# Local and pooled attention with a gated feed-forward on one core: the last product in float16, its scale from a per-batch bound, tails of two batches together, the pooled attention on quadrants of TensorE

## The chip, the cores and the metric

One core of a Trainium2 chip runs the program. The metric is the device time in microseconds (us), the median of several runs. A profile of one execution shows every instruction of its engines: TensorE (PE, with its weight loads PEld), VectorE (DVE), ScalarE (ACT), GpSimd (POOL) and SyncE (SP), which starts the transfers.

## What is computed

Batch B = 8, heads H = 8, sequence S = 576, head dimension D = 64. The attention's output is the input of a gated feed-forward; the outputs of the two attentions are added first.

```python
q_d, k_d, v_d = (mean over 4 neighbouring positions of q, k, v)      # 144 positions
out_up = repeat(softmax(scale * q_d @ k_d.T) @ v_d, 4)               # pooled attention
scores = where(abs(pos[:, None] - pos[None, :]) < 4, scale * q @ k.T, -1e9)
x = out_up + softmax(scores) @ v                                     # local attention
h = maximum(x @ w_in, 0)                                             # 512 -> 1024
u, v = h[..., :512], h[..., 512:]
v_n = (v - mean(v)) / sqrt(var(v) + 1e-6)
v_s = einsum('ts,bsd->btd', w_spatial, v_n) + b_spatial[None, :, None]
out = (u * v_s) @ w_out
```

The weights w_in and w_out come as 64-bit floats and are taken apart as integers on the chip.

## The kernel before

**Two kinds of work.** `attention(n)` handles unit n, a pair of heads of one batch (32 units, four to a batch). `gated(b)` handles the feed-forward of batch b. Neither runs as written: each piece is handed to a planner (`Plan`) as an operation with an engine, an assumed duration, its buffers and a rank. The planner then writes out one fixed order for each engine, and every engine works through its own list in that order. So a changed duration, rank or buffer count moves instructions everywhere. Tables of numbers (`RANK`, `MRANK`, `WRANK`) hold the ranks; `ON` says for each unit which engine does a piece that several can do.

**A unit.** S: the local scores, ten windows of 64 by 64 for each of the two heads, as 20 float32 products that each use one quadrant (64 rows by 64 columns) of TensorE's array (L663). Then mask, maximum, subtraction, exponential, sum and division on VectorE, ScalarE or GpSimd. T turns the probabilities (L716), AV multiplies by v, again 20 products on quadrants (L796). The pooled half: two additions make the sums of four (L631, L634); Sd, the pooled scores, is three float32 products that use the whole array, with the two heads laid out in a matrix padded with zeros (qd, L638, L728); Td turns the probabilities (L764); AVd is four products that use one half of the array's columns each (L782). L806 adds the two attentions into xf, and x is xf split into two float16 parts, high and low (L814, L816).

**A batch's feed-forward.** V (L844, the last 64 rows L849), U (L899) and SP, the spatial product (L917 to L920), are float16 products of 12 to 14 matmuls; each sums high times high, high times low and low times high. g = u * v_s is split into two float32r parts (L930, L924), and O, the last product (L947), is 12 matmuls of 512 columns in float32r for every 128 rows of the output. The last 64 rows of each batch make a product of 8 matmuls of their own (L952): high and low rows stand under each other and two further instructions add them (L959, L960).

**Start.** The weights are decoded by six operations for each of 12 pieces (L453 to L478), their size is bounded (L401 to L415), and they are split (L426, L429). x needs the scale of its batch, which needs all of v of the batch. TensorE has no weights for V until then. Where the planner expects a gap on TensorE in the first 110 us, it fills it with matmuls whose result nobody reads (L985).

Of the kernel before, what the change touches and what calls it, by code (L numbers as in the profile page):

```python
# [23 lines left out]
NW = len(WS)  # L24
# [29 lines left out]
class Op:  # L54
    __slots__ = ("eng", "ns", "fn", "rank", "lag", "port", "kb", "mode", "succ", "wait", "ready", "bufs", "name", "way")
# [14 lines left out]
TURN = {"FQ": 93.0, "FH": 93.0, "QF": 120.0, "QH": 100.0, "HF": 200.0, "HQ": 200.0, "FF": 0.0, "QQ": 20.0, "HH": 0.0}  # L70
# [6 lines left out]
class Plan:  # L77
# [18 lines left out]

    def op(self, eng, ns, fn, r=(), w=(), hold=(), after=(), rank=0.0, lag=None, port=False, kb=0, mode="",
           name=""):
# [8 lines left out]
        o.mode = mode  # L107
# [24 lines left out]
    def run(self, near=150.0, stay=0.0, dma=(1500.0, 4.2, 500.0), emit=True):  # L132
# [4 lines left out]
        moved = 0.0  # L137
        next_of = {t: 0 for t in self.places}
# [10 lines left out]
        while left:  # L149
            best = None  # L150
            for eng, ops in todo.items():
                t0 = free[eng]
                first, found = None, []
                for o in ops:
# [14 lines left out]
                    if ok:  # L169

                        ask = t
# [42 lines left out]
            if o.kb:  # L214
                moved = max(moved, t + dma[0]) + o.kb * dma[1]

                stop = t + dma[0] + 2 * o.kb * dma[1] + 2 * dma[2] if o.eng == "POOL" else moved + dma[2]
# [22 lines left out]
RANK = {"load": [-2.065, -19.673, -22.423],  # L240
        "vload": [14.683, -10.412, -19.503],
        "vabs": [1.439, 2.3, -51.738],
        "tv": [-29.16, -7.708, 15.837],
        "sum": [-11.259, -21.094, 21.557],
        "S": [-37.552, -7.505, 7.145],
        "E": [-6.056, 0.92, -0.304],
        "N": [-1.928, 0.973, 7.716],
        "T": [-13.789, 4.31, -7.205],
        "Sd": [-6.836, 6.538, 1.368],
        "Nd": [-13.355, -14.998, -2.48],  # L250
        "Td": [-12.97, -17.495, 0.215],
        "AVd": [-13.065, -3.029, 0.094],
        "AV": [9.436, 0.605, -3.631],
        "X": [-0.741, 3.256, -1.768]}
# [12 lines left out]
NEAR = 109.698
STAY = 7.379
# [15 lines left out]
def tile_kernel(ctx, tc, qk, vw, v4, w_in, wT, bsp, w_out, out, emit=True):  # L284
# [34 lines left out]
    for par in range(2):  # L319
# [7 lines left out]
    rebias = const.tile([P, 1], F32, name="rebias")  # L327
    nc.gpsimd.memset(rebias, -7.0 * 2.0**30)
# [5 lines left out]


# [7 lines left out]
    plan.tag("g", [const.tile([P, NF, 2 * HN], F32R, name="ga"),  # L343
                   lambda: const.tile([P, NF, 2 * HN], F32R, tag="gb", name="gb")])
# [17 lines left out]
    places("ed", 2, [96, 3, G], F32)
    places("mxd", 2, [P, 3], F32)
    places("smd", 2, [P, 3], F32)
    places("pdT", 1, [72, 2, 3, 96], F32)
# [13 lines left out]
    sw = const.tile([P, 3, 16], F32, name="sw")  # L379
    places("mb", 5, [P, FF], F32)  # L380
    places("wst", NT + 1, [P, S], F32)
    places("bias", 1, [P, S], F32)
    places("row", 5, [P, FF], F32, fifo=False)
    places("u", 5, [P, HN], F32)
# [3 lines left out]
    PEL = 260  # L388

# [4 lines left out]
    def bound(t, k, toks, tok, rank, up, fac, low):  # L394

# [4 lines left out]
        def turn_b():  # L400
            nc.tensor.transpose(pb.ap[:k, :P], t()[:, :k], ident)  # L401

        def greatest():
            nc.vector.tensor_reduce(t()[:k, 10:11], pb.ap[:k, :P], axis=AX.X, op=ALU.max)

        def spread():
            nc.tensor.matmul(pb.ap[:, P:P + 1], ones[:k], t()[:k, 10:11], start=True, stop=True)

        def scales():
            e, sc, iv = (t().bitcast(I32)[:, i:i + 1] for i in (7, 8, 9))  # L410
            nc.vector.tensor_copy(t()[:, 7:8], pb.ap[:, P:P + 1])
# [619 lines left out]
```

## Time and profile before

| | |
|---|---|
| median of 3 runs | 594.53 us (593.16 to 594.92) |
| profiled execution, from the first to the last instruction | 593.0 us |
| TensorE busy | 571.2 us, 96% |
| VectorE / ScalarE / GpSimd busy | 440.1 / 351.3 / 88.1 us |
| TensorE's granted clock, mean | 0.996 of full speed |
| moved by DMA | 56.95 MB |

The profile gives no time for its own execution beside the span; the span is 1.5 us under the median of the runs. Busy time counts overlapping matmuls' durations only once, and a matmul's shown duration is longer than the distance to the next one, because they are pipelined. So what a product costs TensorE is read here from start to start.

### The profile page before, as it was taken

The numbers are of one execution on the slowest core, as the hardware profiler recorded it, in microseconds if no ns is written. First come the engines' busy times: TensorE is split into PE (matmuls) and PEld (weight loads), VectorE is DVE, ScalarE is ACT, GpSimd is POOL, SyncE is SP. The second block draws the span as 40 slices with busy tenths as digits, with TensorE's granted clock in tenths as the row PEclk, the third lists the DMA queues.
The fourth block names the chain that finished last, engine by engine and source line by source line (L and its number), as shares of the span: only waits on it lengthen the run. The fifth ranks groups of instructions, "written<-read, shape, count | busy, mean of one in ns | idle before, by whom it ended". The sixth has DMA issues, their size and how long they took to land.

```text
span 593.0 us, 14813 instructions
## 1 busy us (share of the span) xinstructions
PE 571.2 (96%) x6062; PEld 420.0 (71%) x6062; DVE 440.1 (74%) x1077; ACT 351.3 (59%) x886; POOL 88.1 (15%) x109
## 2 busy tenths in 40 slices
PE   7777899999999999999999999999999999999997
PEld 3444558786788668776888678776787678766775
DVE  5889999987885968796687947797687957554340
ACT  3798998666656465665656555665656445533421
POOL 3212464002200040003100210003100110001100
PEclk9999999999999999999999999999999999999999
DMA  8999714215341623144140442144130110001002
GB/s 271 230 309 238 200 27 99 77 34 155 60 151 38 166 57 122 33 145 102 40 126 34 133 103 98 48 146 88 55 125 10 74 49 34 2 19 45 19 1 80
DMA packets 37383, 56.95 MB, mean 96 GB/s; under 512 B 3650, under 2 KB 24130, under 8 KB 37316
## 3 DMA queue, kind: packets, MB, share of 16 engines
q1 hardware_dynamic: 35012, 48.94, 26.2%
q0 software_dynamic: 2304, 7.08, 7.4%
q8 instruction: 47, 0.77, 0.5%
q14 instruction: 20, 0.16, 0.1%
HBM read 46.57 MB, written 9.44 MB: 94 GB/s over the span
## 4 chain that ended last, share of the span: by engine, by line
PE 84%; DVE 5%; ACT 4%; DMA 3%; issue 2%; POOL 0%; ACTq 0%; DVEq 0%; POOLq 0%
PE pmc L917 4%; PE pmc L844 4%; PE pmd L899 4%; PE pmb L947 4%; PE pmb L917 4%; PE pma L899 4%; PE pmb L844 4%; PE pmd L917 4%; PE pmd L947 4%; PE pmc L947 4%; PE pma L917 4%; PE pmc L899 3%; PE pma L947 3%; PE pmb L899 3%; PE pab L796 2%; PE pma L844 2%
## 5 line engine op out<-in xcount | busy, mean ns | idle before, releaser
L899 PEld LDWEIGHTS <-win 128*128 128x128 f16 x768 | 74.4, 98 | 19.5 <-issue 1.5
L917 PEld LDWEIGHTS <-vha 128*128 128x128 f16 x768 | 73.8, 98 | 19.4 <-issue 1.7
L581 POOL DMA_DIRECT2D tvb<-v_dram x12 | 10.3, 857 | 126.2 <-DMA tvb<-v_dram 102.9
L917 PE MATMUL pmc<-wsp,vha 128*128 128x320 f16 (+1 forms) x204 | 28.6, 290 | 0.0
L985 PE MATMUL pma<-mask_b,mask_a 128*128 128x512 bf16 x91 | 24.7, 417 | 3.2 <-DVE sw L506 3.2
L917 PE MATMUL pmb<-wsp,vha 128*128 128x320 f16 (+1 forms) x192 | 27.1, 291 | 0.0
L581 POOL DMA_DIRECT2D tva<-v_dram x12 | 10.8, 902 | 101.3 <-DMA tva<-v_dram 56.8
L917 PE MATMUL pmd<-wsp,vha 128*128 128x256 f16 (+1 forms) x192 | 24.9, 279 | 0.0
L917 PE MATMUL pma<-wsp,vha 128*128 128x256 f16 (+1 forms) x180 | 24.0, 283 | 0.0
L872 POOL TENSOR_TENSOR sta<-sta,mhalf 128x1 f32<-128x1 f32 (+1 forms) x14 | 11.2, 803 | 78.9 <-DVE sta L856 72.3
L872 POOL TENSOR_TENSOR stc<-stc,mhalf 128x1 f32<-128x1 f32 (+1 forms) x13 | 11.0, 845 | 67.7 <-DVE stc L856 67.5
L676 DVE TENSOR_TENSOR sa<-pab,mask 128x384 f32<-128x384 f32 (+1 forms) x24 | 10.5, 480 | 11.9 <-PE pab L663 11.8
L985 PEld LDWEIGHTS <-mask_a 128*128 128x128 bf16 x97 | 9.4, 104 | 13.8 <-issue 3.6
L704 ACT ACTIVATE sa<-sa 128x640 f32<-128x640 f32 x16 | 11.8, 735 | 11.8 <-DVE sa L682 11.8
L947 PE MATMUL pmd<-wo,ga 128*128 128x512 f32 x72 | 18.1, 399 | 0.0
L947 PE MATMUL pma<-wo,gb 128*128 128x512 f32 x72 | 18.0, 399 | 0.0
L844 PEld LDWEIGHTS <-xa 128*128 128x128 f16 x96 | 9.3, 98 | 11.8 <-issue 1.1
L947 PEld LDWEIGHTS pmd<-wo,ga 128*128 128x128 f32 x72 | 13.3, 188 | 3.0
L947 PEld LDWEIGHTS pma<-wo,gb 128*128 128x128 f32 x72 | 13.3, 188 | 3.0
L947 PE MATMUL pmb<-wo,ga 128*128 128x512 f32 x60 | 15.1, 401 | 0.0
L872 POOL TENSOR_TENSOR stb<-stb,mhalf 128x1 f32<-128x1 f32 (+1 forms) x13 | 10.7, 826 | 23.4 <-DVE stb L856 23.1
L806 DVE TENSOR_TENSOR xfa<-pab,dna 128x232 f32<-128x232 f32 x32 | 11.2, 391 | 2.8 <-ACT win L426 1.7
(730 smaller groups left out, 1653.2 us busy)
## 6 DMA issues: line engine op xcount, KB each, us to landing
qka<-qk_dram SPq DMA_DIRECT2D x16, 576.0 KB, 3.8
qkb<-qk_dram SPq DMA_DIRECT2D x16, 576.0 KB, 6.2
tva<-v_dram POOLq DMA_DIRECT2D x12, 288.0 KB, 4.4
tvb<-v_dram POOLq DMA_DIRECT2D x12, 288.0 KB, 4.4
out_dram<-rowb SPq DMA_DIRECT2D x9, 256.0 KB, 2.0
stg<-w_in_dram SPq DMA_DIRECT2D x4, 512.0 KB, 4.8
more<-w_in_dram SPq DMA_DIRECT2D x4, 512.0 KB, 9.8
out_dram<-rowa SPq DMA_DIRECT2D x7, 256.0 KB, 2.0
```

What stands on the lines that cost most here:

```text
L581: plan.op("POOL", 850, lambda r=r: nc.gpsimd.dma_start(t.ap, v4[b, r], accum_op=ALU.add), w=[t], rank=rank + 2.0 + 0.3 * r, kb=288, name="tv")
L676: nc.vector.tensor_tensor(sv, pv, mask[:, None, None, :].broadcast_to(list(pv.shape)), op=ALU.add)
L704: exp_of.append(plan.op("ACT", 643, lambda: nc.scalar.activation(s.ap, s.ap, AF.Exp, scale=1.0 / 8.0), w=[s], rank=R["E"], name="exp"))
L796: nc.tensor.matmul(pv.ap[h * 64:h * 64 + 64, c:c + QB[w + 1] - QB[w]], vb.ap[k, w], pT.ap[k, blk, q0:q0 + QB[w + 1] - QB[w]], start=True, ...
L806: nc.vector.tensor_tensor(xo[:, :, o], pj[:, o, :m].rearrange("p (j g r) -> p j g r", j=2, r=4), do[:, :, o, :, None].broadcast_to([P, 2, ...
L844: nc.tensor.matmul(ps.ap, xs[c].ap[:, i, t * P:(t + 1) * P], win[:, c, j, FF:], start=(c == 0 and (i, j) == (0, 0)), stop=(c == NC - 1 and ...
L872: plan.op("POOL", 530, lambda: nc.gpsimd.tensor_tensor(st.ap[:r, 8:9], st.ap[:r, 8:9], mhalf[:r], op=ALU.pow), w=[st], rank=rank - EVICT, ...
L899: nc.tensor.matmul(ps.ap[:, :n], win[:, c, i, ft * P:(ft + 1) * P], xs[c].ap[:, j, HA[h]:HA[h + 1]], start=(c == 0 and (i, j) == (0, 0)), ...
L917: nc.tensor.matmul(ps.ap[:, :n], vh.ap[:, c, i, fs], wsp[:, c, j, hs], start=(c == 0 and (i, j) == (0, 0)), stop=False)
L947: nc.tensor.matmul(ps.ap, g.ap[:, c, o1:o1 + P], wo[:, c, j, :], start=(c == 0 and (i, j) == (0, 0)), stop=(c == NF - 1 and i == 1))
L985: nc.tensor.matmul(ap.rearrange("p (j k) -> p j k", k=64), mask_a, mask_b[:, None, :].broadcast_to([P, 8, 64]), start=True, stop=True)
```

## The change

**Last product.** w_out is kept as two float16 parts instead of float32r, and so is g. float16 needs g in a bounded range. A new bound per batch does this: the ReLU that makes u also sums its rows (`accum_out`, L1105), VectorE takes the largest of the eight sums, TensorE turns that column, VectorE takes its maximum, TensorE spreads it over the partitions with a product with ones, and three small VectorE operations make two scales. The gate (L1155) multiplies by one, and the copy of the output (L1174) by the other.

**Tails.** The last 64 rows of g of two batches go into one buffer `gt`, and after every second batch `o_tails` multiplies both by w_out in 12 matmuls.

**Pooled attention.** Sd becomes six products on quadrants, without the padded qd and without its two scaling copies. AVd becomes eight products on quadrants with an addition of the two halves. Td turns 112 instead of 96 columns. From unit 8 on S and Sd are one piece of the plan, and AVd and AV are one.

**Others.** The decoding takes four operations instead of six. For 18 of 32 units the subtraction of the maximum moves into ten exponentials of 64 columns each. More work goes to GpSimd. The sizes of w_spatial's columns are summed by ten matmuls (L642). The first four qk tiles have buffers of their own. All ranks and assumed durations are new, with one rank per batch and, for the first two batches, per unit.

```diff
-    wo = const.tile([P, NF, 2, E], F32R, name="wo")
+    wo = const.tile([P, NF, 2, E], F16, name="wo")
...
-        plan.op("PE", 720, scores_d, r=[kb, qb.sub(0), qb.sub(1)], w=[pd], hold=[ed], rank=R["Sd"], lag=PEL, mode="F", name="Sd")
...
+            q = kb.ap.rearrange("p x g -> p (x g)")
+            for h, a, i, e in ((0, 0, 0, 0), (0, 1, 1, 0), (1, 1, 0, 2), (1, 2, 1, 2), (0, 2, 0, 1), (1, 0, 1, 1)):
+                r, o = slice(h * 64, h * 64 + 64), slice(i * 64, i * 64 + 64)
+                nc.tensor.matmul(third(e)[o], q[r, a * 48:a * 48 + 64], kb.ap[r, 1], start=True, stop=True)
...
+        merge = n >= MERGE
...
+            second = plan.op(Way("mask", n, T=("PE", 1710, False), D=("PE", 1242, False)), 0, lambda: (scores(), scores_d()), r=[qkb, kb], w=[pst, pdt, pe],
+                             hold=[s, ed], rank=R["S"], lag=PEL, mode="Q", name="S")
...
-                    nc.tensor.matmul(pw.ap[h * 64:h * 64 + 64, :G], vd[:, kc * 2 + h, :], t[:, kc, :, h, :],
+            for kc in range(2):
+                for c, h in ((0, 0), (1, 1), (0, 1), (1, 0)):
+                    k = slice(c * 64, KEYS if c else 64)
+                    nc.tensor.matmul(bank(two_w, c ^ h)[h * 64:h * 64 + 64, base[c ^ h]:base[c ^ h] + G], vd[k, kc * 2 + h, :], t[k, kc, h * G:h * G + G],
                                      start=(kc == 0), stop=(kc == 1))
...
+            plan.op("ACT", 480 if h == 0 else 535, lambda: nc.scalar.activation(u.ap[:, :n], ps.ap[:, :n], AF.Relu, scale=iv.ap[:, 1:2], accum_out=au.ap[:, h * NF + ft:h * NF + ft + 1]),
...
+                turned.append(bound(lambda: au.ap, 1, [au.sub(8), ("sw", 2), ("sw", 3)], au.sub(9), rank, scales, 480))
...
-            plan.op("DVE", 341 if h == 0 else 407, lambda: nc.vector.scalar_tensor_tensor(u.ap[:, :n], ps.ap[:, :n], sw[:, 2, 9:10], u.ap[:, :n], op0=ALU.mult, op1=ALU.mult),
-                    r=[ps], w=[u], rank=rank - EVICT, name="gate")
+            plan.op("DVE", 395 if h == 0 else 460, lambda: nc.vector.scalar_tensor_tensor(u.ap[:, :n], ps.ap[:, :n], au.ap[:, 9:10], u.ap[:, :n], op0=ALU.mult, op1=ALU.mult),
+                    r=[ps, au.sub(9)], w=[u], rank=rank - EVICT, name="gate")
...
+        def o_tails():
...
+                for c in range(NF):
+                    for i, j in PAIRS:
+                        nc.tensor.matmul(ps.ap, gt.ap[:, c, i].rearrange("p s t -> p (s t)"), wo[:, c, j, :],
+                                         start=(c == 0 and (i, j) == (0, 0)), stop=(c == NF - 1 and i == 1))
...
-        for ft in range(NF):
-            s_piece(0, ft)
-            u_piece(1, ft)
+        for h in range(2):
+            for ft in range(NF):
+                u_piece(h, ft)
```

TensorE's list, in the middle of a batch before: Td, S of two units, AVd, then SP (pa and pm are accumulators, qk the loaded heads, pdT the turned pooled probabilities, tv the pooled v).

```order
L764 MATMUL pmb<-ident,eda 72x96 x3
L764 MATMUL pma<-ident,eda 72x96 x3
L663 MATMUL pab<-qka 64x64 x20
L663 MATMUL paa<-qkb 64x64 x20
L782 MATMUL pmc<-pdTa,tva 64x144 x4
L917 LDWEIGHTS vha
L917 MATMUL pmd<-wsp,vha 128x256
```

TensorE's list now, in the middle of a batch: AVd, AV, S and Sd of three different units, then O (kd holds the sums of four).

```order
L929 MATMUL pab<-pdTa,tva 64x144 x8
L962 MATMUL pab<-probTa,vf 64x60 x2
L962 MATMUL pab<-probTa,vf 64x58 x2
L962 MATMUL pab<-probTa,vf 64x56 x2
L962 MATMUL pab<-probTa,vf 64x58 x10
L962 MATMUL pab<-probTa,vf 64x54 x2
L962 MATMUL pab<-probTa,vf 64x58 x2
L758 MATMUL paa<-qka 64x64 x20
L820 MATMUL paa<-kdb 64x144 x4
L820 MATMUL pmc<-kdb 64x144 x2
L1170 LDWEIGHTS ga
L1170 MATMUL pmb<-wo,ga 128x512
```

Sd and AVd have joined the pieces on quadrants. Stretches on quadrants or halves, of which there were 42, are now 58 in the whole program: 14 are AVd, AV, S, Sd, ten are AVd, AV, and 21 are one piece alone, most of them in the first two batches. From the first V on, TensorE changes from whole array to parts 31 times before and 36 times now.

VectorE's list at the end of the start, before: the rows up to the low part of the batch's fourth x (xd), for which the first V waits (suma and kda are sums of four, mx maxima, wsp the split w_spatial, mb and row the weights in decoding).

```order
L816 SCALAR_TENSOR_TENSOR xc<-xfa,sxa,xc 128x576
L685 TENSOR_REDUCE mxa<-pab 128x10
L806 TENSOR_TENSOR xfb<-paa,dnb 128x2x116 x2
L808 TENSOR_TENSOR xfb<-paa,dnb 128x112
L691 TENSOR_TENSOR sa<-pab,mxa 128x2x3x64
L691 TENSOR_TENSOR sa<-pab,mxa 128x2x2x64
L732 TENSOR_REDUCE mxda<-pmc 96x3
L463 SCALAR_TENSOR_TENSOR rowc<-more,rowc 128x512
L816 SCALAR_TENSOR_TENSOR xd<-xfb,sxa,xd 128x576
```

VectorE's list at the same place now: from one split of w_spatial over the first three x; xd stands nine rows after the last of these rows.

```order
L514 SCALAR_TENSOR_TENSOR wsp<-wsta,sw,wsp 128x576
L1014 SCALAR_TENSOR_TENSOR xb<-xfb,sxa,xb 128x576
L1014 SCALAR_TENSOR_TENSOR xa<-xfa,sxa,xa 128x576
L514 SCALAR_TENSOR_TENSOR wsp<-wstb,sw,wsp 128x576
L981 TENSOR_TENSOR xfb<-pab,dna 128x2x116 x2
L983 TENSOR_TENSOR xfb<-pab,dna 128x112
L514 SCALAR_TENSOR_TENSOR wsp<-wstc,sw,wsp 128x576
L483 TENSOR_REDUCE sw<-pmb 4x1
L484 TENSOR_SCALAR sw<-sw 4x1
L1014 SCALAR_TENSOR_TENSOR xc<-xfb,sxa,xc 128x576
L981 TENSOR_TENSOR xfa<-paa,dnb 128x2x116 x2
L983 TENSOR_TENSOR xfa<-paa,dnb 128x112
```

All four splits of w_spatial, and those of its last rows and the bias, now stand ahead of xd, where one split stood. In all, 133 instructions of VectorE ended with xd before, and 177 do now. They include the exponentials' sums of six units instead of four and the pooled maxima of seven instead of five.

## Rows read from the trace of the kernel before

**Rows 1.** The page's first part: busy time and instructions of each engine.

```profile
PE 571.2 (96%) x6062; PEld 420.0 (71%) x6062; DVE 440.1 (74%) x1077; ACT 351.3 (59%) x886; POOL 88.1 (15%) x109
```

**Rows 2.** Windows: stretch, length; PE, PEld, DVE, ACT, POOL busy; clock, DMA share, GB/s.

```profile
0.00:66.00 66.00, 50.04 (x623) 29.44 (x624) 54.20 (x132) 49.72 (x129) 19.11 (x33) 0.97 0.89 248
66.00:120.00 54.00, 52.07 (x502) 36.61 (x501) 52.93 (x129) 44.15 (x114) 19.48 (x19) 1.00 0.38 102
120.00:575.00 455.00, 455.00 (x4879) 342.94 (x4878) 330.70 (x813) 253.92 (x639) 49.50 (x58) 1.00 0.26 75
575.00:593.00 18.00, 14.11 (x64) 10.99 (x62) 2.22 (x5) 3.49 (x7) 0.00 (x0) 0.97 0.18 66
```

**Rows 3.** Timeline of PE at the start (start, length), and one group of lines.

```profile
15.05 0.81 PE L663 MATMUL paa<-qka 64*64 64x64 f32 x40
66.03 0.81 PE L844 MATMUL pma<-win,xa 128*128 128x512 f16 x3
L985 PE MATMUL pma<-mask_b,mask_a 128*128 128x512 bf16 x91 | 24.7, 417 | 3.2 <-DVE sw L506 3.2
```

**Rows 4.** Timeline of DVE at the start (start, length; idle before, releaser).

```profile
2.63 0.48 DVE L332 CAST mask_b<-mask 128x64 bf16<-128x64 f32 x1 [2.63 <-POOL mask L323]
...
13.44 0.68 DVE L472 SCALAR_TENSOR_TENSOR mbc<-more,mbc 128x512 f32<-128x512 uint32 x1
14.04 0.42 DVE L453 TENSOR_SCALAR rowd<-more 128x512 int32<-128x512 int32 x1
14.38 0.68 DVE L478 TENSOR_TENSOR mbc<-mbc,rowc 128x512 f32<-128x512 f32 x1
...
65.94 0.82 DVE L816 SCALAR_TENSOR_TENSOR xd<-xfb,sxa,xd 128x576 f16<-128x576 f32 x1 [1.16 <-ACT xd L814]
```

**Rows 5.** The chain that ended last: start, share of it in us, what.

```profile
205.31 2.59 PE pmc L844 x12
581.64 2.80 PE pmd L947 x12
584.44 1.87 PE pmb L952 x8
589.20 0.59 ACT rowc L957
```

**Rows 6.** Timeline of PE in a middle batch (start, length of the group).

```profile
222.66 0.90 PE L728 MATMUL pma<-kda,qda 128*96 128x144 f32 x6
223.49 0.85 PE L796 MATMUL pab<-probTa,vf 64*64 64x60 f32 x38
...
230.44 0.41 PE L764 MATMUL pmd<-ident,eda 96*72 96x96 f32 x3
230.69 0.41 PE L764 MATMUL pmc<-ident,eda 96*72 96x96 f32 x3
231.03 0.81 PE L663 MATMUL pab<-qka 64*64 64x64 f32 x40
231.66 0.76 PE L663 MATMUL paa<-qkb 64*64 64x64 f32 x40
232.35 0.72 PE L782 MATMUL pmd<-pdTa,tvb 72*64 72x144 f32 x8
233.00 0.39 PE L899 MATMUL pmc<-xb,win 128*128 128x256 f16 x2
```

**Rows 7.** Timeline of PE around one batch's bound for x.

```profile
120.51 0.27 PE L401 MATMUL pmb<-ident,sxa 128*4 128x128 f32 x1
120.62 0.90 PE L728 MATMUL pmc<-kda,qda 128*96 128x144 f32 x6
121.35 0.71 PE L716 MATMUL pab<-ident,sa 128*128 128x128 f32 x5
121.99 0.38 PE L407 MATMUL pmb<-sxa,ones 4*128 4x1 f32 x2
122.30 0.98 PE L728 MATMUL pmd<-kdb,qdb 128*96 128x144 f32 x6
```

**Rows 8.** Two lines on one tile: shortest, median, longest in ns, first and last start.

```profile
L634 DVE TENSOR_TENSOR kdb<-suma x14: 436/451/855, 19.9 to 477.6; 128x288 f32<-128x288 f32 x14
L872 POOL TENSOR_TENSOR stc<-stc,mhalf x13: 549/862/1961, 79.7 to 548.0; 128x1 f32<-128x1 f32 x11, 64x1 f32<-64x1 f32 x2
```

More of the change, by code (lines that the diff above doesn't have):

```diff
@@ L95, in buf, with follow @@
         return b
+    def follow(self, ops, after):
+        for o in ops:
+            for p in after:
+                if o not in p.succ:
+                    p.succ.append(o)
+                    o.wait += 1
     def op(self, eng, ns, fn, r=(), w=(), hold=(), after=(), rank=0.0, lag=None, port=False, kb=0, mode="",
-           name=""):
+           name="", lanes=1):
         o = Op()
@@ L406, in spread @@
         def spread():
[L407 to L411, printed above, removed]
-            nc.vector.tensor_scalar(e, e, 0x7F800000, None, op0=ALU.bitwise_and)
-            nc.vector.tensor_scalar(e, e, -1.0, -low * 2.0**23, op0=ALU.mult, op1=ALU.min)
-            nc.vector.tensor_scalar_add(sc, e, (268.0 - up) * 2**23)
-            nc.vector.tensor_scalar(iv, e, -1.0, (up - 14.0 + fac) * 2**23, op0=ALU.mult, op1=ALU.add)
@@ new lines, in bound, with powers @@
+        turned = plan.op("PE", 110, turn_b, r=toks, w=[pb], rank=rank, lag=PEL, mode="F", name="bound")
+        plan.op("DVE", 310, greatest, r=[pb], w=[tok], rank=rank - EVICT, name="great")
+        plan.op("PE", 110, spread, r=[tok], w=[pb], rank=rank, lag=PEL, mode="F", name="spread")
+        plan.op("DVE", cost, lambda: scales(pb.ap[:, P:P + 1]), r=[pb], w=[tok], rank=rank - EVICT, port=True, name="scale")
+        return turned
+    def powers(t, up, fac, low):
+        return lambda most: exponents(t, most, up, fac, low)
@@ L540, in tile_kernel @@
     obits = w_out.bitcast(I32)
+    late, bias = [], []
     wtok = {"WV": [], "WU": [], "WSP": [], "WO": []}
@@ new lines, in columns, with sums, greatest @@
+    def columns(parts):
+        i, k = 2, "WSP"
+        pb = plan.buf("pa")
+        last = WRANK[k + " bound"][-1]
+        sizes, toks = [], []
+        for c, (done, t, n) in enumerate(parts):
+            a = plan.buf("u")
+            sizes.append(a)
+            rank = WRANK[k + " bound"][c]
+            plan.op("ACT", act(n), lambda a=a, t=t: nc.scalar.activation(a.ap.bitcast(BF16)[:, :S], t.ap, AF.Abs), r=[t], w=[a], rank=rank, name="wabs")
+        rows = slice(TAIL, TAIL + 2)
+        plan.op("ACT", act(S), lambda: nc.scalar.activation(sizes[-1].ap.bitcast(BF16)[rows, :S], bias[0].ap[rows, :S], AF.Abs),
+                r=[bias[0]], w=[sizes[-1]], rank=last, name="wabs")
+        hs = S // 2
+        def sums():
+            for c in range(len(parts)):
+                k = P if c < NT else TAIL + 2
+                for h in range(2):
+                    nc.tensor.matmul(pb.ap[:, 512 * h:512 * h + hs], ones_b[:k], sizes[c].ap.bitcast(BF16)[:k, h * hs:(h + 1) * hs],
+                                     start=c == 0, stop=c == len(parts) - 1)
+        def greatest():
+            nc.vector.tensor_reduce(sw[:, i, 7:8], pb.ap.rearrange("p (h c) -> p h c", h=2)[:, :, :hs], axis=AX.XY, op=ALU.max)
+            exponents(lambda: sw[:, i], None, 0.0, -10.0, 50.0)
+        plan.op("PE", 1400, sums, r=sizes, w=[pb], rank=last, lag=PEL, mode="F", name="columns")
+        plan.op("DVE", 1260, greatest, r=[pb], w=[("sw", i)], rank=last - EVICT, port=True, name="scale")
@@ L818, in attention, with hi_up, low_up @@
-        plan.op("ACT", 201, lambda: nc.scalar.copy(xt.ap[:, p], x.ap[:, :, NT * P:]), r=[x.sub(0), x.sub(1)],
+        def hi_up():
+            for o, i in zip(views_x(x.ap[:, 0]), views_p()):
+                nc.scalar.activation(o, i, AF.Copy, scale=sx.ap[:, 8:9])
+        def low_up():
+            for o, i, a in zip(views_x(x.ap[:, 1]), views_p(), views_x(x.ap[:, 0])):
+                nc.vector.scalar_tensor_tensor(o, i, sx.ap[:, 8:9], a, op0=ALU.mult, op1=ALU.subtract)
+        if not merge:
+            before = plan.op("PE", 600, values_d, r=[tv, pdT.sub(0), pdT.sub(1)], w=list(two_w), hold=[xf if up else dn], rank=R["AVd"], lag=PEL, mode="Q", name="AVd")
```

689 lines of the change are left out of this document (421 added, 268 removed).

## Prediction

> **What bounds the kernel now.** I read the page's first part, then windows, then the timeline at the places that the change touches. The first part says that TensorE is busy 96% of the span [rows 1]. The windows say where the other 4% lie [rows 2]. From 120 to 575 us it is busy for all of the 455 us, and at full clock; nobody else counts there, since VectorE is busy for 331 of them and ScalarE for 254. From 66 to 120 us it loses 1.9 us. Up to 66 us it is busy for only 50 of 66, and much of that is filler: by its list the program has 97 filler matmuls, all but five of them before 66.03 us, when the first V starts [rows 3]. From filler to filler it is some 0.26 us (the group's 24.7 us over 91 is 0.27), so 24 us of the start are filler, 16 idle and 26 useful. The end is 3.9 us after TensorE's last product: a copy of 0.59 us [rows 5] and the transfer of the output.
>
> So there are two clocks to read. From the first V on, time is the sum of TensorE's products, start to start. Before it, time is whatever the fourth x of the first batch waits for. That x's low part starts at 65.94 us, 0.09 us before V [rows 3, 4], and VectorE, which makes it, has then been busy for 54.2 of 66 us [rows 2].
>
> **Last product.** Twelve matmuls in float32r take 2.80 us on the chain; twelve in float16 of the same 512 columns take 2.59, shown by V [rows 5]. 32 products times 0.21 are 6.7 us. Tails: 8 times 1.87 [rows 5] become 4 times 2.59, 15.0 to 10.4, so 4.6 less. Sum: −11.3. Nothing hides this or takes it back, as TensorE has no gaps there; I see no reason for a range over 1 us.
>
> **Pooled scores.** Sd takes 0.83 us before a quadrant piece [rows 6], and 0.81 in most other places. 26 of the 32 follow the first V: 21.3 us. New: six products on four quadrants, two in a row on the fullest. The trace has no quadrant product of 144 columns. Lower bound: a float32 product of 144 columns in the whole array is a third of a piece of 0.73 (its shortest distance, after another whole-array piece [rows 7], from 120.62 to 121.35), 0.24; two are 0.49. Upper bound: no gain, 0.81. The nearest row is S: five deep per quadrant, with 64 columns 5 times 0.108 or 0.54 by the same price, and 0.63 measured from S to S [rows 6]. So a piece costs some 0.09 over its depth, and I take 0.58. Leaving the quadrants for the whole array costs something too: S to AVd is 0.69 against 0.63, and I take 0.10 for 22 of them. 24 pieces now follow the first V: 13.9 + 2.2 = 16.1, so −5.2.
>
> By the Trainium skill, TensorEngine Tiling (Array Packing), Tiling Modes, Key Properties, tiles run their loads and matmuls independently of each other. The sum by that alone would be 0.49 for Sd and for the next piece, 4.5 us less in all; the S rows, 0.63 for a depth of 0.54, do not reach it.
>
> **Pooled values.** AVd takes 0.65 [rows 6], leaving included; 28 are 18.2 us. New: eight products, again two deep, 0.58 by the same price and with the same bounds, and no own leaving where AV follows; 26 are 15.1. So −3.1.
>
> **Td, S, mode changes, bounds.** Td goes from 96 to 112 columns: 0.25 for three [rows 6] becomes 0.29; 28 pieces at 0.50 become 25 at 0.58: +0.5. S: one fewer after the first V, and it leaves straight into Sd: −1.4. Changes from whole array into quadrants cost 0.09 in the piece before (Td takes 0.34 before S, 0.25 before Td [rows 6]); counted without those inside the 0.83, 21 become 36: +1.3. Bounds: a turning costs 0.11 and a spread 0.31 as float32 [rows 7]. Eight new turnings are +0.9; the spreads become 16 in one bfloat16 pass, which no row shows: between 0.11 (the turning, also a single pass) and 0.31, I take 0.12: −0.6. Two more masks by matmul, +0.3, and two fewer leavings of AV, −0.3. Together +0.7.
>
> TensorE from the first V on: −11.3 − 5.2 − 3.1 + 0.7 = **−18.9**. The bounds on quadrant pieces move this from −23.4 (both 0.49) to about −7 (both 0.81).
>
> **The wait that is added.** The gate now waits for the bound: ReLU, largest of eight, turning, maximum, spread, scales. TensorE's spread waits for VectorE's maximum, and behind it on TensorE stand all further products. Between turning and spread the list puts two SP pieces, 3.4 us by their matmuls, against some 1.4 us for the chain in between (0.27 of the turning, two short VectorE operations, their signals). So I cost it at nothing; were VectorE's list 2 us late every time, it would be 8 times 2, 16 us.
>
> **The other engines.** VectorE loses 61 operations of 0.6 us and more (18 subtractions, 10 sums of four, 11 normalisations, 14 low parts of v, eight additions of tails) and gains some hundred short ones. ScalarE gains some 30: ten exponentials for one in 18 units, eight sums per batch, 24 pieces of normd, less the 64 copies of qd. That is about 380 of 570 us, still cover for everything while TensorE is full. The U and V evictions stay behind their accumulators as before.
>
> **The start.** Ahead of and with xd, VectorE had 133 instructions and now has 177. By start-to-start distances [rows 4]: 0.60 for a two-tensor operation of 512 elements, 0.34 for one with a scalar. Decoding: 37 operations, 18 us, become 30, 15 us, −3. Splits of w_spatial and the bias stand ahead of xd: +4. Two to three more units' maxima, sums, pooled maxima and reciprocals, and the new additions of the pooled halves: +7. Clearing the new buffers: +3. Less mask and subtraction work: −3. A copy of bounds and exponents: +2. Sum +10, so 64.4 us of work in place of 54.2. How long VectorE idles there has two bounds: 2.6 us, the time to its first instruction [rows 4], so V at 67.0; and the 11.8 of before, V at 76.2. qk is issued earlier and has four buffers, so less waiting than before; but ScalarE, with 49.7 us of work there before [rows 2], now has five units' exponentials in ten parts and two more units' pooled pieces on top, some 10 us, and the two wait for each other. I take 6, V at 70.5: **+4.5**. TensorE's useful work ahead of V is about the same 26 us, so the start is pure delay. The 1.9 us lost from 66 to 120 and the 3.9 of the end I leave as they are.
>
> **Sum.** 593.0 + 4.5 − 18.9 = 578.6 us span. The runs' median is 1.5 above the profiled span; so 580.1, and I say 580.
>
> **The rivals.**
> *The start is free and the quadrants are ideal*: V at 67.0 and both pieces 0.49: 593.0 + 1.0 − 23.4 + 1.5 = 572. For it: VectorE is the only one full there. Against it: S at 0.63. Chance 0.18.
> *The start waits as much as before*: V at 76.2, and the work that VectorE has not finished costs TensorE 3 us more between 66 and 120: 593.0 + 10.2 + 3 − 18.9 + 1.5 = 589. For it: ScalarE's list is also full. Chance 0.17.
> *GpSimd blocks VectorE.* GpSimd gets about 78 us more of work in all. One addition on VectorE of 0.45 us took 0.86 once, and a power on GpSimd of 0.55 took 1.96 once [rows 8]: each waits for the other. From the first V on VectorE has room for it; in the start GpSimd has about 3 us more than the 19 [rows 2], and all of it on top of the forecast gives 583. If VectorE also falls behind the bound, 2 us a batch, it is 599, slower than before; it decides from about 1.7 us a batch. By the Trainium skill, SBUF — State Buffer, Who interferes with whom, VectorE with two SBUF inputs and GpSimd reading SBUF exclude each other for a whole instruction; the doubled durations agree. Chance of 583: 0.12 (inside the forecast's range), of slower: 0.05.
> *The quadrants do not overlap with 144 columns.* Then Sd is 6 times 0.24, 1.46, and AVd 8 times 0.24, 1.94: 50.5 + 35.0 in place of the 29.0 taken, +56, so 636. Against it: S would be 2.2 and is 0.63. It decides from 0.87 a piece, where 50 pieces eat the 14.4 us. Chance 0.03.
>
> **How the numbers follow.** The forecast, with its neighbour at 583, has 0.57; its own range is 576 to 586. With the two outer cases below 594 the range is 570 to 592. A difference of 0.3%, 1.8 us, is what a measurement of this kernel can tell. Faster: 0.57 + 0.18 + most of 0.17 and no other, 0.88. Slower: 0.05 + 0.03, 0.08, and 0.04 between.
>
> **What would show it.** In the profile after: O pieces 2.59 apart; AVd to AV and Sd from S 0.55 to 0.62; the first V at 69 to 72 us with VectorE's list without gaps over 1 us after 20 us; no idle time on TensorE from 120 us on, above all none ahead of the spread L487. The forecast is wrong if V comes after 78 us, if Sd or AVd stay at 0.8, or if TensorE waits for VectorE in the middle batches.

## The result and the profile after

| | before | after |
|---|---|---|
| median, us | 594.32 (593.16 to 594.92, 4 runs) | 586.54 (585.85 to 590.34, 4 runs) |
| ratio to before | | 0.9876, 95% interval 0.9839 to 0.9913 |
| profiled execution, us | 593.0 | 584.7 |
| first V starts at, us | 66.03 | 80.05 |
| from there to the end, us | 527.0 | 504.6 |

The change makes the kernel 7.8 us faster; 14.5 were forecast. The last two rows say where it went: the end comes 22.4 us sooner after the first V (18.9 forecast), and the first V 14.0 us later (4.5 forecast). A second measurement of the same kernel gave 587.73, so a run below is read against 586.5 to 587.7. One of the ten executions of the run no_cover took 953.46 us at a granted clock of 0.56 and is left out of its median.

The page's first part of the kernel after, to be read against [rows 1]: TensorE's share is 95% instead of 96%, VectorE has lost 21 us, ScalarE has gained 24 and GpSimd has doubled.

```profile
PE 557.9 (95%) x6507; PEld 371.5 (64%) x6507; DVE 419.0 (72%) x1106; ACT 375.7 (64%) x1099; POOL 181.5 (31%) x203
```

Windows of the kernel after, cut at its first V (columns as in [rows 2]): from 120 to 575 us TensorE lacks 1.4 us and the clock is full, so the middle is as the forecast wanted it. In the start VectorE is busy for 68.9 of 80 us and the clock's mean is 0.91. The last row is a part of the first: from 62 us to the first V, VectorE is busy for 17.0 and ScalarE for 16.6 of 18.05 us.

```profile
0.00:80.05 80.05, 59.40 (x813) 34.08 (x814) 68.94 (x177) 61.66 (x192) 26.39 (x41) 0.91 0.86 251
80.05:120.00 39.95, 39.34 (x384) 26.37 (x383) 36.30 (x98) 32.94 (x92) 13.28 (x13) 1.00 0.12 32
120.00:575.00 455.00, 453.57 (x5290) 308.74 (x5288) 313.74 (x834) 278.38 (x814) 141.85 (x149) 1.00 0.27 77
62.00:80.05 18.05, 13.58 (x168) 7.25 (x168) 16.98 (x51) 16.59 (x40) 2.49 (x3) 0.91 0.85 209
```

The end of the start in the kernel after: VectorE's low part of xd, and the first V, which waits for it and starts when it ends (a Td of TensorE's own list lasts as long).

```profile
79.30 0.76 DVE L1014 SCALAR_TENSOR_TENSOR xd<-xfa,sxa,xd 128x576 f16<-128x576 f32 x1
```

```profile
80.05 0.81 PE L1039 MATMUL pmb<-win,xa 128*128 128x512 f16 x3
```

The end of the chain that ended last, in answer to [rows 5] (columns as there; SP is L1134 to L1137, the last product L1170): a last product is 2.59 us instead of 2.80, and the tails of two batches are one product of 2.59 (L1185) instead of two of 1.87.

```profile
571.31 1.31 PE pma L1134 x12
572.62 0.11 PE pma L1136
572.73 0.11 PE pma L1137
572.84 2.59 PE pmb L1185 x12
575.43 2.59 PE pmd L1170 x12
578.02 2.60 PE pmc L1170 x12
```

TensorE's timeline in a middle batch of the kernel after, in answer to [rows 6] and [rows 7], from start to start: AVd 0.54 (307.94 to 308.48), AV 0.58 (to 309.06), S 0.65 (to 309.71), Sd 0.64 with its leaving (to 310.35), the bound's spread 0.11 (L487, to 310.46).

```profile
307.94 0.72 PE L929 MATMUL pab<-pdTa,tva 64*64 64x144 f32 x16
308.48 0.80 PE L962 MATMUL pab<-probTb,vf 64*64 64x60 f32 x38
309.06 0.27 PE L758 MATMUL paa<-qka 64*64 64x64 f32 x2
...
309.71 0.28 PE L820 MATMUL paa<-kdc 64*64 64x144 f32 x1
...
310.01 0.41 PE L820 MATMUL pma<-kdc 64*64 64x144 f32 x4
310.35 0.17 PE L487 MATMUL pmb<-aud,ones_b 1*128 1x1 bf16 x1
310.46 1.48 PE L1134 MATMUL pmd<-wsp,vha 128*128 128x256 f16 x12
```

**Where the start stalls.** Four timelines of the kernel after, around 16 us. VectorE's decoding instruction L555, of a kind that takes 0.69 us elsewhere, takes 4.67:

```profile
15.29 0.82 DVE L804 TENSOR_REDUCE sma<-sa 128x10 f32<-128x640 f32 x1 [0.92 <-ACT sa L798]
16.03 4.67 DVE L555 SCALAR_TENSOR_TENSOR mbc<-more,mbc 128x512 int32<-128x512 int32 x1
20.62 0.81 DVE L780 TENSOR_REDUCE mxb<-paa 128x10 f32<-128x640 f32 x1
```

In these us GpSimd makes the sums of four of units 1 and 2, which the change gave to it, one behind the other:

```profile
16.35 1.46 POOL L730 TENSOR_TENSOR sumb<-qkb 128x576 f32<-128x576 f32 x1
17.46 1.44 POOL L730 TENSOR_TENSOR suma<-qkc 128x576 f32<-128x576 f32 x1
18.56 0.96 POOL L733 TENSOR_TENSOR kdb<-sumb 128x288 f32<-128x288 f32 x1
19.19 0.95 POOL L733 TENSOR_TENSOR kdc<-suma 128x288 f32<-128x288 f32 x1
```

ScalarE waits for that instruction:

```profile
20.79 0.63 ACT L658 ACTIVATE junk<-mbc 128x512 bf16<-128x512 f32 x1 [4.45 <-DVE mbc L555]
```

And TensorE waits for ScalarE. It is idle for 4.73 us, and when it starts again at 24.59 its clock is at half, 1.2 GHz, for some us (granted 0.50 from 24.5 to 28 us, 0.77 in the mean of 15 to 30): five products of T take 1.07 us from start to start, 27.02 to 28.09, and 0.54 at full clock, 305.08 to 305.62.

```profile
24.59 0.76 PE L820 MATMUL paa<-kdb 64*64 64x144 f32 x8 [4.73 <-ACT sb L798]
...
27.02 1.27 PE L854 MATMUL pab<-ident,sa 128*128 128x128 f32 x5
28.09 0.76 PE L901 MATMUL pmd<-perm,eda 112*100 112x112 f32 x3
...
305.08 0.71 PE L854 MATMUL paa<-ident,sb 128*128 128x128 f32 x5
305.62 0.45 PE L901 MATMUL pma<-perm,edb 112*100 112x112 f32 x3
```

### The profile page after: what moved, and what is told of

It is laid out like the page before. It is cut to its first block, busy times and chain, and to the rows that moved or that the text cites. A ratio compares the mean times of both kernels' runs of the same rounds, so it can differ in the third digit from the quotient of the medians.

```text
span 584.7 us, 16107 instructions
## 1 busy us (share of the span) xinstructions
PE 557.9 (95%) x6507; PEld 371.5 (64%) x6507; DVE 419.0 (72%) x1106; ACT 375.7 (64%) x1099; POOL 181.5 (31%) x203
## 4 chain that ended last, share of the span: by engine, by line
PE 83%; ACT 5%; DVE 5%; DMA 3%; issue 2%; SPq 1%; ACTq 0%; DVEq 0%
PE pma L1134 5%; PE pmd L1102 4%; PE pmb L1102 4%; PE pmc L1134 4%; PE pmb L1170 4%; PE pmd L1170 4%; PE pmc L1102 4%; PE pmd L1134 4%; PE pma L1170 4%; PE pma L1102 4%; PE pma L1039 4%; PE pmb L1134 3%; PE pmd L1039 3%; PE pmc L1170 3%; PE pmb L1039 3%; PE pmc L1039 3%
## 5 line engine op out<-in xcount | busy, mean ns | idle before, releaser
L1134 PEld LDWEIGHTS <-vha 128*128 128x128 f16 x768 | 73.9, 98 | 18.9 <-issue 0.4
L1170 PEld LDWEIGHTS <-gb 128*128 128x128 f16 x288 | 27.7, 98 | 31.3 <-issue 0.4
L1134 PE MATMUL pma<-wsp,vha 128*128 128x256 f16 (+1 forms) x240 | 32.1, 283 | 0.0
L1134 PE MATMUL pmc<-wsp,vha 128*128 128x256 f16 (+1 forms) x204 | 27.6, 285 | 0.0
L1134 PE MATMUL pmd<-wsp,vha 128*128 128x320 f16 (+1 forms) x168 | 22.9, 286 | 0.0
L1134 PE MATMUL pmb<-wsp,vha 128*128 128x320 f16 (+1 forms) x156 | 22.1, 291 | 0.0
L1170 PE MATMUL pmd<-wo,gb 128*128 128x512 f16 x96 | 22.0, 379 | 0.0
L730 POOL TENSOR_TENSOR sumb<-qkb 128x576 f32<-128x576 f32 x9 | 11.0, 1224 | 30.3 <-DMA qkb<-qk_dram 30.3
L1170 PE MATMUL pmb<-wo,gb 128*128 128x512 f16 x72 | 16.5, 379 | 0.0
L1039 PEld LDWEIGHTS <-xa 128*128 128x128 f16 x96 | 9.4, 98 | 11.1 <-issue 0.5
L1170 PEld LDWEIGHTS <-ga 128*128 128x128 f16 x96 | 9.1, 98 | 10.1 <-issue 0.4
L1170 PE MATMUL pma<-wo,gb 128*128 128x512 f16 x60 | 13.8, 379 | 0.0
L1170 PE MATMUL pmc<-wo,gb 128*128 128x512 f16 x60 | 13.8, 379 | 0.0
```

The costliest lines, as they stand in the source:

```text
L730: side(s1).tensor_tensor(sb.ap.rearrange("p x (g r) -> p x g r", r=2), x[:, :, :, :2], x[:, :, :, 2:], op=ALU.add)
L1039: nc.tensor.matmul(ps.ap, xs[c].ap[:, i, t * P:(t + 1) * P], win[:, c, j, FF:], start=(c == 0 and (i, j) == (0, 0)), stop=(c == NC - 1 and ...
L1134: nc.tensor.matmul(ps.ap[:, :n], vh.ap[:, c, i, fs], wsp[:, c, j, hs], start=(c == 0 and (i, j) == (0, 0)), stop=False)
L1170: nc.tensor.matmul(ps.ap, g.ap[:, c, HA[1] * i + k:HA[1] * i + k + P], wo[:, c, j, :], start=(c == 0 and (i, j) == (0, 0)), stop=(c == NF ...
```

## The experiments

Each kernel differs from the changed one as its diff shows, f16_alone from the one before. The ratios are to the kernel before in the same call. In several runs pieces are moved by hand: the plan's order is recorded, and then the pieces named (kind and running number) are written out right behind another one. Nothing else in the lists moves. The first V stands at 79.38 to 80.05 in the three runs whose start is that of the change (after, after_again, no_cover), so a difference of less than about 1 us there says nothing.

| run | median, us | ratio, 95% interval | first V at, us |
|---|---|---|---|
| after_again | 587.73 | 0.9889 (0.9859 to 0.9918) | 79.72 |
| sums_on_vector | 584.27 | 0.9827 (0.9805 to 0.9850) | 77.01 |
| one_exp | 587.60 | 0.9889 (0.9862 to 0.9915) | 80.56 |
| wsp_low_zero | 588.51 | 0.9890 (0.9851 to 0.9929) | 80.94 |
| sizes_late | 589.21 | 0.9903 (0.9880 to 0.9926) | 80.03 |
| sums_sizes | 590.30 | 0.9921 (0.9892 to 0.9949) | 76.91 |
| splits_late | 592.09 | 0.9963 (0.9940 to 0.9986) | 75.78 |
| scale_early | 590.90 | 0.9932 (0.9911 to 0.9952) | 85.06 |
| all_three | 598.49 | 1.0065 (1.0047 to 1.0083) | 83.47 |
| no_cover | 590.67 | 0.9941 (0.9917 to 0.9965) | 79.38 |
| same_quadrant | 587.72 | 0.9888 (0.9859 to 0.9917) | 78.96 |
| f16_alone | 588.21 | 0.9895 (0.9868 to 0.9922) | 64.92 |

> The changed kernel once more, beside the two runs of this call: 586 to 587 in every theory.

It gave 587.73, 0.7 us above that.

**sums_on_vector.**

```diff
-            side(s1).tensor_tensor(sb.ap...
+            (nc.vector if n < 3 else side(s1)).tensor_tensor(sb.ap...
-            side(s2).tensor_tensor(kb.ap, ...
+            (nc.vector if n < 3 else side(s2)).tensor_tensor(kb.ap, ...
```

> The sums of four of units 1 and 2 (four GpSimd operations between 16 and 20 us) are done by VectorE at the same places of the order; nothing else moves. Theory (VectorE's list paces the start, and these four operations lengthened one of its instructions from 0.69 to 4.67 us): that instruction falls back to 0.7, VectorE has 1.9 us more work, so the first V comes some 2 us earlier, at 78, and the time is 584.5; up to 4 us earlier if TensorE's halved clock around 25 us goes with it. Rival (ScalarE or the transfers pace the start, the 4 us are absorbed): first V at 80 to 82, time 586.5 to 588.

The theory's 584.5 was met: 584.27, the best kernel of the study. VectorE's timeline around the same instruction (0.68 now, with one of the sums behind it) and TensorE's row of the first V, 3.04 us earlier than after's:

```profile
16.34 0.68 DVE L555 SCALAR_TENSOR_TENSOR mbc<-more,mbc 128x512 int32<-128x512 int32 x1
16.94 0.77 DVE L730 TENSOR_TENSOR suma<-qkc 128x576 f32<-128x576 f32 x1
```

```profile
77.01 0.60 PE L1039 MATMUL pmb<-win,xa 128*128 128x512 f16 x2
```

**one_exp.**

```diff
-        plan.op(sb2, 0, less_a if late_max else less_p if pe_mask else less, ...
+        plan.op(sb2, 0, (less_p if pe_mask else less) if n < 5 or not late_max else less_a, ...
-        ... exp_a if late_max else exp_s, ...
+        ... exp_a if late_max and n >= 5 else exp_s, ...
```

> In units 0 to 4 VectorE subtracts the maximum again and ScalarE does one exponential in place of ten. ScalarE has 5 times 1.5, 7 us, less in the start, VectorE 5 times 0.75, 3.7 us, more. Theory (VectorE paces): first V some 3.7 us later, at 83 to 84, time 590. Rival (ScalarE paces): first V 4 to 7 us earlier, at 73 to 76, time 580 to 583.

Neither. By the trace ScalarE is busy for 5.9 us less ahead of the first V and VectorE for 4.2 us more; that moves the first V by 0.5 us and the time by nothing that can be told. So neither list alone sets the pace of the start. The run changes both engines at once, so it can't tell whether two effects cancel.

**wsp_low_zero and sizes_late**, the pair that relieves one engine each.

```diff
-                lambda: nc.vector.scalar_tensor_tensor(dst_lo, src(), scale, dst_hi, ...),
+                lambda: nc.vector.memset(dst_lo, 0.0) if key[0] == "WSP" else nc.vector.scalar_tensor_tensor(...),
-        ... nc.vector.scalar_tensor_tensor(wsp_lb[:TAIL], t.ap[:TAIL], sc[:TAIL], wsp_hh[:TAIL], ...)
+        ... nc.vector.memset(wsp_lb[:TAIL], 0.0)
```

> The low part of w_spatial is left out: five subtractions of 0.81 us on VectorE ahead of the first V become five memsets of some 0.2 us, which fill the low part with zeros; all else stays. Theory (VectorE's list paces): first V some 3 us earlier, at 77, time 583.5. Rival (they stand in gaps of VectorE's list, the start waits for something else): first V at 80, time 586.5.

```diff
+MOVES = [(["vabs.4"], "wabs.17"), (["vabs.5"], "relu.3"), (["vabs.6"], "wabs.15"), (["vabs.7"], "vtmp.0"),
+         (["bound.5"], "U.6"), (["great.5"], "great.2"), (["spread.5"], "U.7"), (["scale.6", "inv2.2", "inv2.3"], "wlo.13")]
```

> The list of the changed kernel, but the sizes of the second batch's four v (ScalarE, 0.9 us each, two of them ahead of the first V) and the bound made of them are moved to 92 to 106 us, where ScalarE has some 4 us free; the first x that needs them starts at 108.6. Only ScalarE is relieved ahead of the first V, by 1.8 us, against the run in which only VectorE was, by 3 us, with no gain. Theory (ScalarE's list ends last between 62 us and the first V): first V 1.5 to 1.8 us earlier, at 78.3, time 585. Rival (VectorE's list does, or only both together count): first V at 80, time 586.5.

Both rivals hold in the main: 1.8 us less on ScalarE alone leave the first V at 80.03, and some 2.5 us less on VectorE alone (the memsets take 0.30) leave it at 80.94. In this last run xd is ready at 79.43, 0.6 us earlier than in the kernel after, and the first V did not wait for it: TensorE's own pieces ahead of it ran at half clock (granted 0.50 from 78 to 82 us), after an idle time of 1.75 us up to 75.23. So most of what VectorE was spared, not all, was lost to waiting. (The times are no price of either: in the first the granted clock between 75 and 90 us was 0.77, in the second the moved bound costs the wait named below.)

```profile
78.67 0.76 DVE L1014 SCALAR_TENSOR_TENSOR xd<-xfa,sxa,xd 128x576 f16<-128x576 f32 x1
```

**sums_sizes** is sizes_late and sums_on_vector together.

> The same, and the sums of units 1 and 2 on VectorE. If the two gains are independent (the sums act at 16 to 20 us, the sizes at 70 to 76): 582.5 to 583, first V at 75.5. If the sums alone count: 584.3, first V at 77.

The first V is where the sums alone put it, 76.91, but the time is 6 us above sums_on_vector: between 90 and 120 us TensorE is busy for 27.5 us, there for 29.6. The moved bound is a new wait there: in sizes_late, where its place is the same, the view of waits has 1.4 us of TensorE for it (tile sxb). Behind its waits TensorE's clock was at half (granted 0.50 from 108 to 112 us), which it was not in sums_on_vector. Waits and half clock together make the difference, 4.5 us in the profiled executions.

**splits_late.**

```diff
+MOVES = [(["hh0", "lb0"], "relu1"), (["bh0", "lb1"], "urelu1"), (["whi9", "wlo9"], "relu2"),
+         (["whi8", "wlo8"], "urelu3"), (["whi10", "wlo10"], "relu3"), (["whi11", "wlo11"], "urelu5")]
```

> The list of the changed kernel, but the eleven pieces that split w_spatial and the bias (4.9 us on ScalarE, 5.4 us on VectorE between 64 and 77 us) are moved behind the first V products, between 83 and 97 us, still ahead of the first SP, which needs them. Theory (ScalarE and VectorE are both full from 62 us to the first V): first V 4 to 5 us earlier, at 75 to 76; a part comes back, since both are nearly full up to 110 us too, so 582.5 to 585. Rival (the start ends with a chain through the batch's scale at 71 us, whatever stands beside it): first V at 79 to 80, time 586 to 588.

The first V came 4.3 us earlier, as the theory said; the time did not follow. Windows, and the chain's place in the view of waits (engine, tile and line, releaser, us in total, times, longest): between 90 and 105 us TensorE is busy for 10.1 of 15 us, and waits 4.9 us for the sizes of w_out, which ScalarE now reaches later. From 105 to 110 us its clock is then granted at 0.56.

```profile
75.00:90.00 15.00, 13.55 (x91) 8.24 (x86) 12.63 (x35) 13.90 (x36) 3.11 (x5) 1.00 0.31 68
90.00:105.00 15.00, 10.08 (x60) 5.84 (x58) 13.12 (x26) 9.47 (x24) 6.41 (x5) 0.92 0.00 0
```

```profile
PE pmd L505 <- ACT junk L683: 4.9, 1, 4.9
PE pmb L512 <- DVE sxb L509: 1.2, 1, 1.2
```

**scale_early and all_three.** In the kernel before the turning of the first batch's bound for x stands at 35.80 us, in the kernel after at 64.84 (TensorE's timelines, before and after):

```profile
35.80 0.27 PE L401 MATMUL pmd<-ident,sxa 128*4 128x128 f32 x1 [0.32 <-ACT junk L598]
```

```profile
64.84 0.27 PE L480 MATMUL pmd<-ident,sxa 128*4 128x128 f32 x1 [1.25 <-ACT junk L696]
```

```diff
+MOVES = [(["v2", "v3"], "fetch12"), (["vabs2", "vabs3"], "vabs1"),
+         (["bound3", "great3", "spread3", "scale4", "xhi1", "xlo1", "xhi0", "xlo0", "xtail1", "xtail0"], "wlo0")]
```

Here and in all_three, and for the second batch's bound in sizes_late and sums_sizes, the moved bound's products use columns of accumulator paa that no other piece uses.

> The list of the changed kernel with pieces moved by hand, none added: the loads of the third and fourth v of the first batch are issued some 4 us earlier, their sizes follow on ScalarE right behind the second's (48 us in place of 60 to 64), the batch's bound and scale follow at about 52 in place of 71, and the first two x behind them. Theory (from 60 us on the start is a chain through the batch's scale, which the change made 33 us later; VectorE's work is not what ends last there): the work of xb and xa leaves the crowded stretch from 71 to 76 us, and the first V comes 2 to 3 us earlier, at 77 to 78, time 584. Rival (VectorE's list paces the whole start; it has as many instructions as before): first V at 80, time 586.5.

all_three is scale_early, splits_late and sums_on_vector together.

> The two moves of the runs beside this one, and the sums of units 1 and 2 on VectorE. Theory (three causes one behind the other): their gains add up, 2.3 for the sums as measured, 2.5 for the scale and 2 to 4 for the splits, so 578 to 580, first V at 69 to 71. Rival (all three remove the same wait): 583 to 584, as with the sums alone.

All expectations failed. Moved as one block, the pieces wait for each other (ScalarE idles 1.5 us for the scale ahead of the first x and 0.84 us ahead of a copy of the second), and in ScalarE's list everything behind them waits too. TensorE's waits between 40 and 86 us in scale_early: 4.4 us for a copy of turned probabilities (L884) that now stands on ScalarE behind the two x.

```profile
PE paa L779 <- ACT probTb L884: 4.4, 1, 4.4
PE pmb L508 <- ACT junk L686: 3.3, 1, 3.3
```

So these two say that this block was put badly, not what the late scale costs; all_three carries the same block.

**no_cover.**

```diff
+MOVES = [(["great4", "spread4"], "bound4"), ..., (["great18", "spread18"], "bound18")]
```

> The list of the changed kernel, but TensorE's spread of each batch's new bound stands right behind its turning, so that no SP pieces lie between the two. Theory of the prediction (the added wait is hidden by these pieces and costs about 1.1 us where they are gone; two of the eight batches have hardly any already): 5 to 7 us slower, 592 to 593. Rival (the wait is hidden in any case, because the pieces behind it have slack): 586.5.

Slower, by 2.9 to 4.1 us rather than 5 to 7. TensorE's waits from 200 us on: 0.5 us ahead of each of the six spreads (L512), where the kernel after has none; two of the six rows are shown. With 0.6 us at the batch that had little cover, that makes 3.9 us of waits.

```profile
PE pmd L512 <- DVE auc L509: 0.5, 1, 0.5
PE pmc L512 <- DVE aue L509: 0.5, 1, 0.5
```

**same_quadrant.**

```diff
-            for h, a, i, e in ((0, 0, 0, 0), (0, 1, 1, 0), (1, 1, 0, 2), (1, 2, 1, 2), (0, 2, 0, 1), (1, 0, 1, 1)):
+            for h, a, i, e in ((0, 0, 0, 0), (0, 2, 0, 1), (1, 2, 1, 2), (1, 0, 1, 1), (0, 1, 1, 0), (1, 1, 0, 2)):
```

> The changed kernel, but the six products of Sd are issued in another order: the two that use one quadrant stand one behind the other, instead of four on four quadrants and then two. The work is the same. Theory (TensorE starts its instructions in order, so a second product on a busy quadrant holds back those behind it; quadrants overlap by the order of issue): Sd becomes three deep instead of two, 0.24 us more for each of 32 pieces, so 6 to 8 us slower, 593 to 595. Rival (each quadrant works through its own products independently): Sd stays at 0.6, time 587.

The rival holds: the piece that took 0.64 us in the timeline above takes 0.63, 309.61 to 310.24, and the time is that of after_again.

```profile
309.61 0.48 PE L820 MATMUL paa<-kdc 64*64 64x144 f32 x8
309.85 0.46 PE L820 MATMUL pma<-kdc 64*64 64x144 f32 x4
310.24 0.17 PE L487 MATMUL pmb<-aud,ones_b 1*128 1x1 bf16 x1
```

**f16_alone**, on the kernel before. It leaves out the scaling to float16's range.

```diff
-    return ap.bitcast(F32)
+    return ap
...
-    wo = const.tile([P, NF, 2, E], F32R, name="wo")
+    wo = const.tile([P, NF, 2, E], F16, name="wo")
...
-    plan.tag("g", [const.tile([P, NF, 2 * HN], F32R, name="ga"), ...
+    plan.tag("g", [const.tile([P, NF, 2 * HN], F16, name="ga"), ...
```

> The kernel before with one part of the change alone: w_out and g in float16 in place of float32r, in the same order of work (its scaling to float16's range is left out). By the prediction's price, 32 products of 12 matmuls at 2.59 in place of 2.80 are 6.7 us less and 8 tails of 8 matmuls at 1.73 in place of 1.87 are 1.1 less: 586.4 against 594.3. Rival (the product is limited by what it waits for, not by its type): no gain, 594.

Measured 6.7 us less (interval 4.6 to 7.9), where 7.8 were expected; in its trace the time from the first V on is 7.9 us shorter. The timeline shows 1.73 for the tails and 2.59 for the product ahead of them:

```profile
573.00 2.75 PE L947 MATMUL pmd<-wo,ga 128*128 128x512 f16 x12
575.59 1.89 PE L952 MATMUL pmb<-wo,ga 128*128 128x512 f16 x8
577.32 2.75 PE L947 MATMUL pma<-wo,gb 128*128 128x512 f16 x12
```

## Why the prediction was right, and where it was not

The time moved the way forecast and lies in the outer range (570 to 592), 0.5 us above the forecast's own (576 to 586). Each gain named is in the trace. By one of the prediction's own signs, a first V after 78 us, the forecast of the start was wrong. That the time came no further off than 6.5 us is partly luck: two errors of opposite sign make up most of it, 9.5 us too little for the start and 3.5 too little gain behind it.

**TensorE from the first V on: −18.9 forecast, −22.4 measured.** The sums below are start to start, added up by line over the whole timeline of TensorE from the first V on.

| term | forecast | before | after | measured |
|---|---|---|---|---|
| last product and tails | −11.3 | 107.0 | 94.4 | −12.6 |
| Sd | −5.2 | 21.1 | 14.7 | −6.4 |
| AVd | −3.1 | 18.2 | 14.4 | −3.8 |
| everything else, waits and the last copy too | +0.7 | 380.8 | 381.1 | +0.4 |

No record of these lines is missing; a wait, or a change between whole array and quadrants, falls to the piece ahead of it. The chain's rows say that the first term was priced rightly, 2.80 to 2.59 and two of 1.87 to one of 2.59, and f16_alone, with 7.9 us for the float16 part against 7.8, agrees. Sd and AVd were priced 0.58; AVd came out at 0.54 in the row above and Sd close to its price (0.64 with the leaving, against 0.58 and 0.10). The numbers of pieces behind the first V were right: 24 Sd and 26 AVd. So the 3.5 us lie mostly in what pieces cost on average: a last product 2.87 before, where it was priced 2.80 (15 of the 32 took 2.80, most others 2.88 to 3.00 with what followed); Sd 0.61 after with its leaving, where 0.58 and 0.10 were added; AVd 0.55 in place of 0.58.

**The added wait: right in size, and in part for another reason.** Ahead of the batches' spreads TensorE waits 0.8 us in all, and no_cover shows the cover at work: without it 0.5 us at each of the six that had it. The chain from turning to spread takes 0.82 us where nothing stands between, less than the 1.4 assumed. But the pieces in between are SP in two of the eight batches only; in three they are AVd, AV, S and Sd, as in the timeline above, in one a piece of O, and two batches have little or no cover (waits of 0.3 and 0.5 us, at 110 and 175 us).

**The start: +4.5 forecast, +14.0 measured. This is the step that failed**, and in it the sentence "I take 6" for VectorE's idle time. The work was sized well in sum: 68.9 us busy less the 4.0 by which one instruction was lengthened are 64.9, against 64.4 (the terms listed there add up to 64.2). Idle are 11.1 us, about the 11.8 of before, the outer bound that the prediction kept for a rival; 5.3 of them lie ahead of 16 us, 4.8 between 16 and 62, and 1.1 behind. 64.9, 4.0 and 11.1 make the 80.05. So two rivals were right together, each in part: the start waits as much as before (without the 3 us of later waits that went with it: TensorE lacks 0.6 us from 80 to 120), and GpSimd blocks VectorE. For the second, sums_on_vector settles the cause: with the four GpSimd operations gone the instruction is back at 0.68, the first V comes 2.4 to 3.0 us earlier, net of some 2 us of added VectorE work, and the time falls by 2.3 to 3.5 us. sums_sizes against sizes_late shows it once more: 0.68 in place of 4.67, and the first V 3.1 us earlier. By the Trainium skill, SBUF — State Buffer, Who interferes with whom, an instruction of VectorE with two SBUF inputs and a GpSimd instruction that reads SBUF exclude each other; the trace agrees, with 4.67 us in place of 0.68. The prediction looked for this in one-operation delays of about 0.4 and 1.4 us [rows 8] and priced the start's share at 3, the work that GpSimd would have there beyond the 19 us; it had 7.3 more, 26.4.

For the first, the bookkeeping of VectorE's work and idle time is not a cause. wsp_low_zero takes work from VectorE and its idle time grows instead, 13.7 us for 11.1; sizes_late takes some from ScalarE and nothing comes earlier; splits_late takes from both and the first V comes 4.3 us earlier. Both engines are nearly full from 62 us on, and a piece there counted for much only where it left both. The three runs move different pieces, so that the two engines' waits for each other are the reason is an inference, not shown.

The reading that all this rests on, that the first V waits for the low part of xd, holds in the kernel after; the rows of the kernel before do not show it. There V starts while that part is still being made (65.94 to 66.76) and needs xd only at 67.97; what stood ahead of V was an Sd that had waited for a copy of ScalarE. VectorE, too, waited for ScalarE ahead of xd [rows 4]. So before, VectorE's list did not pace the end of the start, though the prediction priced the start by it.

```profile
65.25 0.95 PE L728 MATMUL pmb<-kdb,qdb 128*96 128x144 f32 x6 [1.15 <-ACT qdb L638]
...
67.97 0.81 PE L844 MATMUL pma<-win,xd 128*128 128x512 f16 x3
```

**"So the start is pure delay" was wrong as well.** From start to start, without idle time, TensorE's useful pieces ahead of the first V are 25.8 us before and 32.8 after; filler and waits are 40.2 and 47.2. Of the 14.0 us, 7.0 are lost and 7.0 are pieces done earlier or at half clock. Over the whole span that makes 14.3 us less useful work (545.6 to 531.3) and 5.9 us more filler and waiting: 8.4 us, the difference of the spans. splits_late shows the same from the other side: an earlier first V is worth nothing where the pieces behind it are not ready.

**Open.** How much the batch's later scale (64.84 instead of 35.80) costs was not told apart, since moving it early by hand made waits of its own. Whether another order of the start could keep the first V at 76 us without the wait at 90 to 105 was not found either.

## What to carry to other kernels

Before giving GpSimd work in a stretch that VectorE paces, look what VectorE does at that place: a run of GpSimd operations can hold one VectorE instruction for the whole run. When two engines feed each other, do not price a start as one engine's work plus a guessed idle time: take the idle time of before as the likely value (11.8 and 11.1 us here), and expect little from relieving one of the two alone where both lists are full. And check in the rows that the milestone waits for what you price, not that the two merely stand side by side. Count time by useful work, filler and waits over the whole span, not by a milestone such as a first product, which work done earlier or later moves as well.

## What the runs showed of the hardware

VectorE's instruction of 0.68 us with two SBUF inputs was held for 4 us, through four GpSimd operations in a row, and not for one of them; it had started 0.32 us ahead of the first. In one_exp and after_again the same place took 4.58 and 4.68 us. In wsp_low_zero and no_cover it started 0.7 and 0.8 us behind the first and was held all the same, for 3.66 and 3.54 us in all. GpSimd's times in a profile are rough, so who asked first can't be told from 0.32 us. Elsewhere the delay was shorter: the same instruction at 98.22 us took 1.53 us and went in behind one GpSimd operation, though a second followed, and an x at 467.62 took 2.33 in place of 0.76, through two. Why it was four in the start is open.

```profile
98.22 1.53 DVE L555 SCALAR_TENSOR_TENSOR mba<-more,mba 128x512 int32<-128x512 int32 x1
```

```profile
97.70 1.50 POOL L1073 TENSOR_TENSOR vha<-rowb,vha 128x512 f16<-128x512 f32 x1 [1.98 <-ACT vha L1071]
99.17 1.70 POOL L846 TENSOR_TENSOR sa<-sa,smc 128x640 f32<-128x640 f32 x1
```

Two products in a row on one quadrant did not hold back the products of other quadrants behind them: 0.63 us for six products in either order. By the Trainium skill, TensorEngine Tiling (Array Packing), Tiling Modes, Key Properties, tiles work independently; this pair of runs agrees.
